# Two of four blocks of x brought in by columns and normalised there by GpSimd, in an attention and MLP block on one core

## The chip, the core and the metric

The kernel runs on one core of a Trainium2 chip. The time is the device time of one execution in microseconds (us). TensorE (PE in the profile, its weight loads PEld) multiplies matrices, VectorE is DVE, ScalarE is ACT, GpSimd is POOL, and SyncE (SP) issues nearly all DMAs. Each engine works through its own instructions in program order and waits on semaphores.

## The reference

x has 2048 rows (tokens) of 448. Cut to what matters:

```python
mod = (silu(c) @ w_mod).reshape(1, 6, 1, 448)          # sa, ca, ga, sb, cb, gb
h = layernorm(x) * (1 + ca) + sa
q, k, v = split_heads(h @ wqkv)                        # 16 heads of 28
p = softmax(q @ k.T * 28 ** -0.5)
x = x + ga * ((p @ v) @ wo)
h = layernorm(x) * (1 + cb) + sb
x = x + gb * (gelu(layernorm(h) @ w1 + b1) @ w2 + b2)  # 448 -> 1792 -> 448
```

Everything is float32. The kernel makes products of nearly that precision out of three faster ones: each operand is split into a rounded part `hi` and a remainder `lo`.

## The kernel before

The work has three stages. The first (to about 163 us) takes x in four blocks of 512 rows. It normalises a block, turns it so that the 448 features lie on partitions, scales and shifts it there by per-partition columns, splits it into hi and lo, and multiplies it with wqkv. The second (163 to 788 us) is attention, in 256 steps; the third is the MLP.

**The turn of a block.** `ln1_stages` (L266) gives eight pieces of work for a block: four take the statistics of 128 rows each on VectorE (`ln_stat`, L208: BN_STATS and BN_AGGR, the last followed by small operations on VectorE and GpSimd), four normalise 128 rows each on ScalarE (L243, L244). Then `h_chunk` (L300) does one of four chunks of 128 features: four TensorE transposes into the PSUM buffer `o` (L287), one ScalarE operation that scales and shifts from there (L308), a ScalarE cast to hi (L292), and a subtraction for lo on GpSimd (L294, L296).

**The tasks of the first stage.** The loop over blocks b runs a list of tasks. A task is eleven matmuls (L407) into one of two `pa` buffers: a group of q or k columns (512 wide), or 128 rows of v (448 wide). ScalarE empties `pa`. After a task's matmuls TensorE runs some products for the softmax's row maxima (L487: 28 rows of q and k, 512 columns), because the attention stage needs each row's maximum before it starts on that row. Each product goes into a PSUM buffer, and VectorE takes its maximum (L492) and so frees it. `mx_ring` hands out these buffers in a fixed cycle of five: ma, ma, m2, m2, m1. A product therefore waits until VectorE is done with the product five places earlier.

**How many products a task gets** is set by `p1_n`. In blocks 1 to 3 a task has five VectorE operations, less those that `emit_mid` (L731) takes. Some of these operations are pairs (`pair_diff`, L496): two products, a Relu on ScalarE (L500) from the first, and one combined VectorE operation (L504, shown as CUSTOM_DVE or ISA) that reads the second. With a pair in the task and `p1_n[1]` true there is one operation more, and the product in the fifth place goes into the buffer `o`. `p1_n[1]` is false where the transposes need `o`. In four tasks of block 1 and one of block 2, `emit_mid` puts four products in the middle of the eleven matmuls. What is not done in the first stage is done in the second, beside the scores.

**Times of the tasks.** I name a task by the microsecond at which its first matmul starts in the trace. Block 1's loop holds eleven tasks, from 55.08 to 97.20. Those with a middle (57.57, 65.30, 73.78, 81.96) have eight products, the others from 61.92 on five or six. The transposes for block 2 stand in the tasks 69.98 to 81.96, those for block 3 in 111.13 to 121.90.

**SP's queue.** SP stores hi and lo of every q and k group to DRAM and copies some rows there (L453, L389), in program order.

## Time and profile before

| | |
|---|---|
| median of three runs | 1090.24 us (1089.82 to 1091.26) |
| the profiled execution, its own time | 1090.18 us |
| its span in the trace | 1088.4 us |
| TensorE busy | 1080.0 us (99%) |
| VectorE, ScalarE, GpSimd busy | 801.5, 696.8, 231.9 us |
| first score matmul of the attention stage | 163.2 us |
| last one starts | 787.9 us |

The profiled execution is 0.06 us below the median. Its span is 1.8 us shorter than its time, for what lies around it. Rows of a timeline give start, length, engine, line, operation, tiles and count; in brackets stands the idle time of the engine before it and what ended it. Rows of windows give, for a stretch A:B, its length and each engine's busy time with its count of instructions. TensorE counts as busy while any of its pipelined matmuls is under way, so a short stall shows less in PE than in the distance between two starts.

### The profile page before, as it was taken

The page shows a single profiled execution, that of the slowest core. Times are in us where ns is not written, and L with a number is a line of the kernel's source. Part 1 is how long each engine was busy: PE and PEld are TensorE (multiplying, and loading weights), DVE is VectorE, ACT ScalarE, POOL GpSimd, SP SyncE. Part 2 cuts the span into 40 slices and gives each one's busy share as a digit, 9 for nine tenths or more (in the row PEclk, how much of TensorE's full clock was granted, in tenths as well). Part 3 has the DMA queues.
Part 4 walks back from the last instruction along what each step waited for, and adds up shares of the span by engine and source line. Part 5 has one row for each costly group of instructions (what it writes and reads, how often), then busy time and mean ns, then how long its engine had stood idle before and what let it go on. Part 6 is the DMA issues. An engine that isn't in the chain of part 4 may idle for free.

```text
span 1088.4 us, 20665 instructions
## 1 busy us (share of the span) xinstructions
PE 1080.0 (99%) x8231; PEld 658.8 (61%) x8231; DVE 801.5 (74%) x1369; ACT 696.8 (64%) x883; POOL 231.9 (21%) x215
## 2 busy tenths in 40 slices
PE   8999999999999999999999999999999999999998
PEld 6766775444444444444444444544388888888887
DVE  6979788999999989988888988584745565464322
ACT  4665658888888888888888888687943321211211
POOL 1543330011011011024231410216114032061000
PEclk9999999999999999999999999999999999999999
DMA  9342272122121202143322423111343311002000
GB/s 312 134 155 76 86 208 88 41 67 58 50 78 59 77 28 58 56 120 87 103 68 77 131 65 96 58 31 59 117 126 96 102 37 41 33 35 73 34 1 34
DMA packets 58870, 88.56 MB, mean 81 GB/s; under 512 B 13807, under 2 KB 25734, under 8 KB 58762
## 3 DMA queue, kind: packets, MB, share of 16 engines
q1 hardware_dynamic: 58290, 86.51, 25.8%
q8 instruction: 64, 1.05, 0.4%
q10 hardware_dynamic: 148, 0.46, 0.1%
q0 software_dynamic: 336, 0.28, 0.1%
q14 instruction: 32, 0.26, 0.1%
HBM read 59.39 MB, written 29.50 MB: 82 GB/s over the span
## 4 chain that ended last, share of the span: by engine, by line
PE 98%; DMA 1%; DVE 1%; ACT 0%; issue 0%; SPq 0%; ACTq 0%
PE s L1393 24%; PE o L1348 24%; PE m L407 17%; PE pa L407 9%; PE m L487 8%; PE s L1485 3%; PE s L1487 3%; PE s L1486 3%; PE s L487 2%; PE t L1487 1%; PE t L1485 1%; PE t L1486 1%; DMA slot_c<-in_w_mod_dram 1%; PE o L287 1%; DVE mxp L492 0%; PE ma L487 0%
## 5 line engine op out<-in xcount | busy, mean ns | idle before, releaser
L492 DVE TENSOR_REDUCE mxp<-m 128x1 f32<-128x512 f32 x553 | 358.1, 686 | 65.0 <-PE m L487 47.7
L1393 PE MATMUL s<-slot_b,slot_a 28*128 28x512 f32 (+1 forms) x3072 | 357.8, 425 | 0.0
L1393 PEld LDWEIGHTS s<-slot_b,slot_a 28*128 28x128 f32 (+1 forms) x3072 | 210.7, 183 | 175.5 <-ACT slot_c L1406 96.4
L487 PE MATMUL m<-kh,qh 28*128 28x512 f32 x606 | 225.8, 469 | 0.8 <-DVE mxp L492 0.3
L1406 ACT ACTIVATE slot_c<-s 128x1024 f32<-128x1024 f32 x170 | 174.8, 1028 | 51.5 <-PE s L1393 50.5
L1348 PE MATMUL o<-slot_c,v 128*32 128x512 f32 x680 | 178.8, 605 | 0.0
L1441 ACT ACTIVATE full<-m,b_col 128x512 f32<-128x512 f32 x56 | 38.6, 690 | 194.2 <-PE m L407 190.0
L698 DVE TENSOR_REDUCE mxp<-s 128x2 f32<-128x1024 f32 x107 | 131.2, 1226 | 5.0 <-PE s L1393 0.3
L1348 PE MATMUL o<-slot_c1h,v 128*32 128x512 f32 x512 | 134.7, 605 | 0.0
L1348 PE MATMUL o<-slot_c0h,v 128*32 128x512 f32 x508 | 133.6, 605 | 0.0
L1406 ACT ACTIVATE slot_c0h<-s 128x1024 f32<-128x1024 f32 x127 | 130.7, 1029 | 0.0
L1406 ACT ACTIVATE slot_c1h<-s 128x1024 f32<-128x1024 f32 x128 | 130.7, 1021 | 0.0
L1406 ACT ACTIVATE slot_d<-s 128x1024 f32<-128x1024 f32 x86 | 88.4, 1028 | 26.1 <-PE s L1393 25.8
L487 PEld LDWEIGHTS m<-kh,qh 28*128 28x128 f32 x606 | 90.4, 182 | 15.4 <-DVE mxp L492 12.7
L1444 DVE CAST hi<-full 128x512 fp32r<-128x512 f32 x42 | 19.2, 458 | 102.0 <-ACT full L1441 101.9
L1068 POOL TENSOR_TENSOR osb<-osb,osb 128x512 f32<-128x512 f32 x16 | 20.6, 1285 | 343.6 <-DMA osb<-drec 282.3
L1348 PE MATMUL o<-slot_d,v 128*32 128x512 f32 x344 | 90.5, 605 | 0.4 <-ACT osb L1312 0.4
L1445 DVE TENSOR_TENSOR lo<-full,hi 128x512 fp32r<-128x512 f32 x56 | 46.2, 825 | 29.7 <-ACT hi L1444 25.7
L407 PE MATMUL m<-y,slot_a 128*128 128x512 f32 x160 | 59.7, 389 | 0.0
L662 DVE CUSTOM_DVE_ANT_0 slot_d0i<-m,slot_d0i 128x512 f32<-128x512 f32 x55 | 38.0, 691 | 16.6 <-PE m L487 14.3
L1348 PEld LDWEIGHTS o<-slot_c,v 128*32 128x32 f32 x680 | 24.5, 108 | 39.7 <-issue 37.8
L492 DVE TENSOR_REDUCE mxp<-ma 128x1 f32<-128x512 f32 x61 | 39.5, 681 | 11.6 <-PE m L487 7.2
(358 smaller groups left out, 1847.1 us busy)
## 6 DMA issues: line engine op xcount, KB each, us to landing
slot_b<-d SPq DMA_DIRECT2D x32, 256.0 KB
slot_a<-d SPq DMA_DIRECT2D x32, 256.0 KB
d<-lo SPq DMA_DIRECT2D x28, 256.0 KB
d<-hi SPq DMA_DIRECT2D x16, 256.0 KB
osb<-drec SPq DMA_DIRECT2D x15, 256.0 KB
out_dram<-xn SPq DMA_DIRECT2D x16, 224.0 KB
raw<-in_B_w_dram SPq DMA_DIRECT2D x14, 224.0 KB
qh<-d SPq DMA_DIRECT2D x12, 256.0 KB
```

Source lines behind the costliest of these rows:

```text
L407: pe.matmul(p, a, b, start=(i == 0), stop=(i == len(terms) - 1))
L487: pe.matmul(m, qh_sb[(g, qt)][js, i * 128 : (i + 1) * 128], k[js, :], start=True, stop=True)
L492: dve.tensor_reduce(out=mxp[(g, qt)][:, i, j, cch : cch + 1], in_=m, op=ALU.max, axis=AX.X)
L698: dve.tensor_reduce(out=mxp[(g, qt)][:, i, j : j + 2, cch], in_=t, op=ALU.max, axis=AX.X)
L1348: pe.matmul(o[32 * j : 32 * j + 32, :], v_sb[kt // 4][:, kt % 4, 4 * g + j, :], p[j // 2][:, j % 2, :], start=(kt == 0), stop=(kt == NKT - 1),
L1393: pe.matmul(s2[:, jj, :], ks[rows_, kp, kc], qs[rows_, qp, :], start=(term == 0), stop=(term == 2))
L1406: act.activation(pt[hf], s2, AF.Exp, scale=SCALE)
L1441: act.activation(gf, p, AF.Gelu_apprx_tanh, bias=b1_col[:, i : i + 1])
L1445: dve.tensor_tensor(out=glo, in0=gf, in1=f(ghi), op=ALU.subtract)
L1485: pe.matmul(pp, ghi[:, ts], w_hi, start=(m == 0), stop=False)
L1486: pe.matmul(pp, ghi[:, ts], w_lo, start=False, stop=False)
L1487: pe.matmul(pp, glo[:, ts], w_hi, start=False, stop=(m == NFT - 1))
```

## The change

Blocks 2 and 3 no longer go through row-wise normalising and transposes. The host hands these rows in a second time, already turned (`x_cols`, feature by feature). The statistics are still taken by rows on VectorE, but two to five tasks earlier in the order. A 128x32 tile of means and reciprocal deviations is turned by one VectorE transpose, sent to DRAM in four small stores, and read back as two tiles in which every partition holds the row of 512 means or deviations. GpSimd then subtracts and multiplies, chunk by chunk (two operations of 128x512 each), in the tasks `APPLY_AT` of the block before. The scaling on ScalarE reads that tile instead of PSUM. As `o` is free of transposes, `p1_n[1]` is true throughout blocks 1 to 3.

```diff
+APPLY_AT = (0, 2, 4, 5)
+    def load_x_cols(b, k):
+        t = xn_t()
+        x_cols[(b, k)] = t
+        if k < 3:
+            sp.dma_start(t, x_t[b - 2, 128 * k : 128 * k + 128, :])
+        else:
+            for h in range(2):
+                sp.dma_start(t[64 * h : 64 * h + 64], x_t[b - 2, 384:D, :])
...
+    def ln1_cols(b):
+        def stat(t):
...
+            ln_stat(mv[0], t, acc[b][:, t, :])
+            if t == 3:
+                st = st32[b % 2]
+                dve.tensor_copy(st[:, 0:4], mv[0][:, :, 0])
+                ve = sbt("ve", [128, 4], bufs=2)
+                dve.tensor_scalar(out=ve, in0=mv[0][:, :, 1], scalar1=EPS, scalar2=None, op0=ALU.add)
+                pool.tensor_tensor(out=st[:, 4:8], in0=ve, in1=neg_half, op=ALU.pow)
+        def rows_out():
+            r = sbt("r32", [128, 32], bufs=2)
+            dve.transpose(r, st32[b % 2])
+            dst = ln_dr[b % 2].rearrange("c (t p) -> (c t) p", p=128)
+            for i in range(4):
+                sp.dma_start(dst[:, 32 * i : 32 * i + 32], r[32 * i : 32 * i + 8, :])
+            for c_ in range(2):
+                sp.dma_start(mr_row(b, c_), ln_dr[b % 2, c_][None].broadcast_to([128, 512]))
+        def apply(k):
+            y = x_cols[(b, k)]
+            pool.tensor_tensor(out=y, in0=y, in1=mr_row(b, 0), op=ALU.subtract)
+            pool.tensor_tensor(out=y, in0=y, in1=mr_row(b, 1), op=ALU.mult)
...
-            p1_n[1] = not (more and (0 <= k < NC)) and not (b == 1 and n < 4)
+            p1_n[1] = bool(b)
...
-                if b and n < 4:
-                    stages[n](xs_next)
+                if b in (1, 2) and n in APPLY_AT:
+                    cols_of[b + 1][1][APPLY_AT.index(n)]()
                 if 0 <= k < NC:
-                    post.append(h_chunk(b + 1, xs_next, k))
-                if later and 7 <= n < 11:
-                    later[n - 7](None)
+                    post.append(h_chunk(b + 1, xs_next, k, x_cols.get((b + 1, k))))
+                n_stat = n - (5, 2, 99)[b]
+                if 0 <= n_stat < 5:
+                    cols_of[b + 2][0][n_stat]()
+                for c_ in {0: range(NC) if n == 10 else (), 1: range(max(0, k - 2), k - 1) if k < NC + 2 else ()}.get(b, ()):
+                    load_x_cols(b + 2, c_)
...
+    x_cols = np.asarray(A_x)[0].reshape(NB, 128, 4, D).transpose(0, 3, 2, 1).reshape(NB, D, 512)[2:]
...
+    nc = bacc.Bacc("TRN2", target_bir_lowering=False, num_devices=1, dynamic_dma_scratch_size=8192)
```

How the order of instructions moves shows at three places. Line numbers of the changed kernel are its own: L492 becomes L549, L504 becomes L561, L487 becomes L544, L407 becomes L464, L210 and L211 become L214 and L215.

The first is VectorE in block 1: all of the task 61.92 and the four middle reductions of the task 65.30. `mxp` holds the maxima; `ma`, `m2`, `m1` and `o` are the PSUM buffers read; the ISA rows are the pair's combined operation. Before:

```order
L492 TENSOR_REDUCE mxp_93_428<-ma_194_842 128x1
L492 TENSOR_REDUCE mxp_93_428<-m2_195_845 128x1
L492 TENSOR_REDUCE mxp_93_428<-m2_196_848 128x1
L504 ISA slot_d0h_15_98,mxp_183_800<-m1_197_851,slot_d0h_15_98 128x512
L504 ISA mxp_183_800 128x1
L492 TENSOR_REDUCE mxp_93_428<-ma_203_873 128x1
L492 TENSOR_REDUCE mxp_93_428<-ma_204_876 128x1
L492 TENSOR_REDUCE mxp_93_428<-m2_205_879 128x1
L492 TENSOR_REDUCE mxp_93_428<-m2_206_882 128x1
```

The same place on VectorE now, in the changed kernel:

```order
L549 TENSOR_REDUCE mxp_97_433<-m2_201_861 128x1
L549 TENSOR_REDUCE mxp_97_433<-m2_202_864 128x1
L549 TENSOR_REDUCE mxp_97_433<-m1_203_867 128x1
L561 ISA slot_d0h_19_102,mxp_190_819<-ma_204_870,slot_d0h_19_102 128x512
L561 ISA mxp_190_819 128x1
L549 TENSOR_REDUCE mxp_97_433<-o_205_873 128x1
L214 BN_STATS st_210_883<-acc3_24_108 128x6
L215 BN_AGGR mv_209_882<-st_210_883 128x2
L549 TENSOR_REDUCE mxp_97_433<-ma_212_898 128x1
L549 TENSOR_REDUCE mxp_97_433<-m2_213_901 128x1
L549 TENSOR_REDUCE mxp_97_433<-m2_214_904 128x1
L549 TENSOR_REDUCE mxp_97_433<-m1_215_907 128x1
```

One reduction (from `o`) and a statistics pair for block 3 now stand ahead of the middle reductions.

The second is TensorE at the end of the task 78.48 and the start of the next, before (`xn` are normalised rows, `pa` the task's result, `ident` the unit matrix):

```order
L487 MATMUL m2_242_1028<-raw_188_814,osb_75_351 128x512
L487 MATMUL m2_243_1031<-raw_188_814,osb_75_351 128x512
L487 MATMUL m1_244_1034<-raw_188_814,osb_75_351 128x512
L487 MATMUL ma_245_1037<-kh0_83_374,qh1_165_717 128x512
L287 MATMUL o_246_1041<-ident_1_77,xn_177_767 128x128
L287 MATMUL o_246_1041<-ident_1_77,xn_191_818 128x128
L287 MATMUL o_246_1041<-ident_1_77,xn_201_858 128x128
L287 MATMUL o_246_1041<-ident_1_77,xn_214_907 128x128
L407 MATMUL pa_248_1050<-slot_e0_34_140,slot_c0_119_523 128x448
```

The same place on TensorE now:

```order
L544 MATMUL ma_256_1068<-raw_91_403,osb_182_783 128x512
L544 MATMUL ma_257_1071<-raw_196_836,osb_79_356 128x512
L544 MATMUL m2_258_1074<-raw_196_836,osb_79_356 128x512
L544 MATMUL m2_259_1077<-kh0_87_379,qh1_173_737 128x512
L544 MATMUL o_260_1080<-raw_91_403,osb_182_783 128x512
L464 MATMUL pa_265_1099<-slot_e0_38_144,slot_c0_125_532 128x448
```

Four transposes are gone, and a product into `o` has come.

The third is VectorE in block 0, the task 33.26 and the first reductions of the task 36.84. Before:

```order
L492 TENSOR_REDUCE mxp_93_428<-m2_112_507 128x1
L492 TENSOR_REDUCE mxp_93_428<-m1_113_510 128x1
L492 TENSOR_REDUCE mxp_93_428<-ma_114_513 128x1
L492 TENSOR_REDUCE mxp_93_428<-ma_115_516 128x1
L446 CAST hi_116_519<-full_117_520 128x512
L492 TENSOR_REDUCE mxp_93_428<-m2_126_556 128x1
```

The same place on VectorE now, from the statistics that stand ahead of it:

```order
L214 BN_STATS st_116_495<-acc2_23_107 128x6
L215 BN_AGGR mv_115_494<-st_116_495 128x2
L503 CAST hi_112_488<-full_113_489 128x512
L549 TENSOR_REDUCE mxp_97_433<-m2_118_516 128x1
L549 TENSOR_REDUCE mxp_97_433<-m1_119_519 128x1
L549 TENSOR_REDUCE mxp_97_433<-ma_120_522 128x1
L549 TENSOR_REDUCE mxp_97_433<-ma_121_525 128x1
L214 BN_STATS st_131_543<-acc2_23_107 128x6
L215 BN_AGGR mv_115_494<-st_131_543 128x2
L503 CAST hi_122_528<-full_123_529 128x512
L549 TENSOR_REDUCE mxp_97_433<-m2_133_568 128x1
```

Block 2's first two statistics pairs have moved here; before, they stood behind the tasks 36.84 and later.

## The prediction

> **What bounds the kernel now.** The page first: the span, who is busy, and the chain of waits that ended last.

> ```profile
> span 1088.4 us, 20665 instructions
> PE 1080.0 (99%) x8231; PEld 658.8 (61%) x8231; DVE 801.5 (74%) x1369; ACT 696.8 (64%) x883; POOL 231.9 (21%) x215
> PE 98%; DMA 1%; DVE 1%; ACT 0%; issue 0%; SPq 0%; ACTq 0%
> ```

> TensorE carries the chain almost throughout, so a TensorE instruction that goes should shorten the kernel. But the page is an average, and a pipelined engine can look busy while it waits. So I read the windows next, cut at the starts of the tasks of the first stage; the columns are length, then busy time (and count) of PE, PEld, DVE, ACT and POOL.

> ```profile
> 61.92:65.30 3.38, 3.38 (x17) 2.28 (x16) 2.01 (x6) 2.35 (x6) 1.02 (x1) 1.00 0.59 213
> 65.30:69.98 4.68, 4.68 (x20) 2.65 (x19) 4.68 (x9) 2.72 (x6) 1.57 (x2) 1.00 0.44 163
> 61.92:69.98 8.06, 8.06 (x36) 4.92 (x35) 6.69 (x14) 5.07 (x11) 2.58 (x2) 1.00 0.50 184
> 69.98:78.48 8.50, 8.44 (x44) 5.71 (x43) 7.09 (x15) 5.93 (x12) 4.11 (x5) 1.00 0.46 170
> 78.48:86.91 8.43, 8.10 (x45) 5.71 (x44) 6.85 (x15) 4.91 (x9) 2.57 (x2) 1.00 0.21 32
> 86.91:90.00 3.09, 3.09 (x20) 2.29 (x18) 2.34 (x7) 1.53 (x3) 1.15 (x1) 1.00 0.21 26
> 90.00:100.94 10.94, 10.94 (x53) 7.38 (x51) 10.87 (x23) 4.76 (x9) 2.71 (x3) 1.00 0.26 90
> 104.37:107.76 3.39, 3.39 (x19) 2.28 (x18) 2.51 (x7) 3.21 (x8) 1.53 (x2) 1.00 0.41 156
> 111.13:121.90 10.77, 10.77 (x62) 8.01 (x60) 7.91 (x17) 8.55 (x17) 6.42 (x8) 1.00 0.46 168
> 121.90:130.30 8.40, 8.23 (x43) 5.50 (x41) 7.42 (x15) 5.20 (x11) 2.57 (x2) 1.00 0.01 3
> 728.53:742.39 13.86, 13.86 (x105) 8.88 (x101) 8.89 (x20) 8.09 (x10) 4.60 (x4) 1.00 0.01 2
> 742.39:746.76 4.37, 4.37 (x32) 2.67 (x32) 0.79 (x4) 2.48 (x3) 3.40 (x3) 1.00 0.03 6
> ```

> In block 1 a plain task (61.92) leaves VectorE free for over a third of its 3.38 us, while a task with products in its middle (65.30) has VectorE busy for all of its 4.68. The timeline of these two shows who ends what.

> ```profile
> 61.92 1.20 PE L407 MATMUL pa<-slot_c,slot_a 128*128 128x512 f32 x4
> ...
> 64.64 0.50 PE L487 MATMUL ma<-raw,qh 28*128 28x512 f32 x1
> ...
> 65.21 0.69 DVE L492 TENSOR_REDUCE mxp<-ma 128x1 f32<-128x512 f32 x1 [1.37 <-PE m L487]
> ...
> 67.02 0.68 DVE L504 CUSTOM_DVE_ANT_0 slot_d0h<-m,slot_d0h 128x512 f32<-128x512 f32 x1
> ...
> 67.62 1.28 DVE L492 TENSOR_REDUCE mxp<-ma 128x1 f32<-128x512 f32 x2
> ...
> 68.82 1.28 DVE L492 TENSOR_REDUCE mxp<-m 128x1 f32<-128x512 f32 x2
> ...
> 69.56 0.50 PE L487 MATMUL m<-kh,qh 28*128 28x512 f32 x1
> 69.98 1.21 PE L407 MATMUL pa<-slot_c,slot_a 128*128 128x512 f32 x4
> ```

> VectorE starts 3.29 after the plain task does (65.21 - 61.92), takes one product each 0.60 (four by 67.62), then the middle's. The last product of the task with a middle goes into the buffer of the middle's third product, counted five back in the cycle. That one's reduction starts at 68.82 and ends 0.68 later; the product follows at 69.56, the next task 0.42 after it. So two tasks take 3.29 + 4 x 0.60 + (2 x 0.60 + 0.68) + 0.48 = 8.05; the window says 8.06. **In block 1 VectorE's in-order work sets the pace, not TensorE's.** The chain puts that stretch down to TensorE all the same.

> **The change part by part.** The sum is made against the profiled execution, 1090.18 us, which is 0.06 below the median of the runs.

> First, VectorE in block 1. In each plain task `p1_n[1]` adds a reduction, in each task with a middle a product at the end, which now needs the buffer of the middle's fourth product. That is 2 x 0.60 per two tasks. The first task with a middle (57.57) begins with VectorE idle and pays one step, +0.6. The statistics, too, come earlier; their price is the start of BN_STATS to that of the next reduction:

> ```profile
> 45.86 0.62 DVE L210 BATCH_NORM_STATS2 st<-acc 128x6 f32<-128x448 f32 x1
> ...
> 46.61 1.25 DVE L492 TENSOR_REDUCE mxp<-ma 128x1 f32<-128x512 f32 x2
> ```

> 0.75 each. Those in the tasks 61.92 and 69.98 stand ahead of the middle's reductions and cost it in full; those behind the tasks with a middle fall where VectorE waits for the next products. So the pair of tasks from 61.92 takes 8.05 + 1.20 + 0.75 = 10.0, **+1.9** on 8.06. The pair from 69.98 has the same list, 10.0, against 8.50: **+1.5**. It loses transposes on the way; their price:

> ```profile
> 77.66 0.50 PE L487 MATMUL ma<-kh,qh 28*128 28x512 f32 x1
> ...
> 78.09 0.66 PE L287 MATMUL o<-ident,xn 128*128 128x128 f32 x4
> ...
> 78.51 1.06 PE L407 MATMUL pa<-slot_e,slot_c 128*128 128x448 f32 x4
> ```

> 0.42 for four, on the path behind a middle, beside VectorE's work elsewhere. The pair from 78.48 has no statistics now but the 128x32 transpose (0.2, as other small operations), and as v tasks are 0.3 shorter it comes to 3.0 + 3.0 + 0.2 + 1.8 + 0.68 + 0.48 = 9.2, **+0.7** on 8.43. The three tasks from 90.00 lose their statistics and should take 3.39 each, as 104.37 does with the same six products: 10.2, **-0.8** on 10.94. Block 1 in sum: 0.6 + 1.9 + 1.5 + 0.7 - 0.8 = **+3.9**. Bounds: +2.4 if the two statistics found a gap after all, +4.6 if the last three tasks gained nothing.

> Second, block 0. There VectorE is just ahead of TensorE's need, and two statistics pairs move in front of these reductions (the tasks 33.26 and 36.84):

> ```profile
> 37.34 1.27 DVE L492 TENSOR_REDUCE mxp<-m 128x1 f32<-128x512 f32 x2
> ...
> 38.54 1.27 DVE L492 TENSOR_REDUCE mxp<-ma 128x1 f32<-128x512 f32 x2
> ...
> 39.28 0.50 PE L487 MATMUL m<-kh,qh 28*128 28x512 f32 x3
> ```

> With one pair ahead, the third reduction (38.54) starts at 39.29 and ends at 39.97. The fourth product of 36.84 reuses that buffer and is due at 39.3: a stall of 0.7. The second pair adds a few tenths in the two tasks after. I take **+1.1**, between 0 (the lag is absorbed) and 1.5 (two pairs in full).

> Third, block 2. Its transposes stand in plain tasks, where TensorE does set the pace. The three tasks 111.13 to 121.90 become one like 104.37 and two like 86.91: 3.39 + 2 x 3.09 = 9.6 against 10.77, **-1.2**, though each does one product more. The stretch from 121.90 gains nothing: its second task has a middle, the reductions before it stay four, and 8.4 is the sum of the first part again (3.0 + 2.4 + 4 steps). ScalarE: a second Relu per task,

> ```profile
> 65.18 0.60 ACT L500 ACTIVATE slot_d0h<-ma 128x512 f32<-128x512 f32 x1 [1.03 <-PE m L487]
> ```

> gives 8.55 + 3 x 0.60 = 10.35 in 9.6, so it ends up to 0.8 late; I take **+0.3**, between 0 and 0.8. The 16 normalising operations that ScalarE loses lie mostly ahead of this and are worth nothing by themselves: ScalarE is busy 5.93 of 8.50 us at most in block 1.

> Fourth, attention. The ten products done earlier end the row maxima sooner, in the steps with a projection: three steps with products take 13.86, one without takes 4.37, so 13.86 - 3 x 4.37 = **-0.75** (0 to -1.2, with one more step beside them).

> Fifth, what is hidden. GpSimd gets 16 operations; a two-input operation of 128x512 there costs

> ```profile
> L1068 POOL TENSOR_TENSOR osb<-osb,osb 128x512 f32<-128x512 f32 x16 | 20.6, 1285 | 343.6 <-DMA osb<-drec 282.3
> ```

> 1.285 each, 20.6 in all, 2.6 per chunk. GpSimd is busy 2.57 to 4.11 of each 8.4 us in block 1, and a chunk is applied two to four tasks ahead of its use: zero. SP issues 22 more DMAs; behind the loads that wait for the rows are only stores that are read tens of us later: zero. The smaller descriptor scratch meets three GpSimd DMAs that follow one on another: zero.

> Sum: 3.9 + 1.1 - 1.2 + 0.3 - 0.75 = **+3.35**, so 1090.18 + 3.35 = **1093.5 us**.

> **The rivals.** *A, TensorE's saving comes through.* If VectorE caught up everywhere, eight groups of four transposes (0.42) and 0.75 in attention would go: 1090.18 - 3.4 - 0.75 = 1086.0. For it speaks the chain (PE 98%), and that six products cost TensorE no more than five (104.37: 3.39, 61.92: 3.38); against it the DVE column at 65.30. Chance 0.13.

> *B, they cancel.* The statistics find gaps (block 0 +0, block 1 +2.4): 3.35 - 1.1 - 1.5 = +0.75, 1090.9. Chance 0.15.

> *C, GpSimd's queue stalls on the rows.* The first chunk's subtraction is queued ahead of the clearing of `mxp` (61.44), for which VectorE's pair operations wait.

> ```profile
> 58.11 1.29 POOL L450 TENSOR_TENSOR lo<-full,kh 128x512 fp32r<-128x512 f32 x1
> ...
> 61.44 0.15 POOL L484 MEMSET mxp<- 128x64 f32 x1
> ```

> ```profile
> osb<-drec POOLq DMA_DIRECT2D x1, 256.0 KB, 6.3
> den<-osb POOLq DMA_DIRECT2D x1, 8.0 KB, 3.7
> ```

> It decides whether the rows have landed by 59.4, when GpSimd is free. The statistics are turned at about 51 (four reductions from 46.61, some 1.6 late); stores and loads at 3.7 and 6.3, with 1.2 of issue, land at about 62. At 6.3 for both it would be 65, the clearing 2.6 + 1.3 later, at 69, and VectorE would lose about 4: 1097.5. [...] Chance 0.08.

> *D, GpSimd and VectorE hold each other up.*

> ```profile
> 29.28 0.42 DVE L446 CAST raw<-full 128x512 fp32r<-128x512 f32 x1
> ...
> 29.37 1.47 POOL L450 TENSOR_TENSOR lo<-full,osb 128x512 fp32r<-128x512 f32 x1
> ```

> Beside a VectorE cast a subtraction took 1.47, not 1.29. If each of the 16 cost VectorE as much, 16 x 0.18 = 2.9 would come on top: 1096.4. [...] Chance 0.05.

> That the change does not do what it says is no rival: the order shows the 32 transposes gone.

> **How the numbers follow.** The forecast has 0.59; its own range, from its terms' bounds, is 1090.5 to 1096. About 0.2% (2.2 us, so 1088.1 and 1092.4) is what can be told from no change. Faster: A, 0.13. Same: B and the low end of the forecast, 0.15 + 0.10 = 0.25. Slower: 0.49 + C + D = 0.62. The range 1088.5 to 1097.0 leaves out A and most of C, 0.2 together.

> **What would show it.** Right: between the starts of the tasks that were 57.57 and 90.00 the changed profile takes some 4.7 us more, tasks with a middle last about 6 us with VectorE busy throughout, the three tasks of block 2 last 9.6, and the maxima end at the step before the projections. Wrong: tasks with a middle under 5 us with VectorE idle in them (A or B), a VectorE wait on GpSimd's clearing near 64 (C), or reductions longer than 0.7 beside GpSimd's work (D).

## The result and the profile after

| | before | changed |
|---|---|---|
| median of six runs each | 1090.0 us (1089.8 to 1091.26) | 1098.3 us (1096.37 to 1100.07) |
| ratio, with its 95% interval | | 1.0074 (1.0061 to 1.0087) |
| the profiled execution, its own time | 1090.18 us | 1100.07 us |
| its span | 1088.4 us | 1098.3 us |
| first score matmul of attention | 163.2 us | 170.9 us |

Slower, as forecast, but by 8.3 us and not by 3.35: 1098.3 lies above the range, which ended at 1097.0. The profiled execution is the slowest of its six. The six differ in the mean clock that TensorE was granted:

| run, us | 1096.37 | 1097.13 | 1097.68 | 1098.91 | 1099.15 | 1100.07 |
|---|---|---|---|---|---|---|
| mean clock | 0.999 | 0.998 | 0.998 | 0.996 | 0.996 | 0.994 |

In the fourteen profiles of this document a mean of 0.998 or less goes with at least one stretch of half clock in the middle of the kernel (a drop, from here on), and 0.999 or 1.000 with none. By that reading five of these six executions have a drop. Of the 68 executions of the kernel before that were run beside the experiments none has: all have 0.999 or 1.000.

The page of the changed kernel gives a row for the clock, in tenths by 40 slices, and the chain of waits:

```profile
PE 1088.0 (99%) x8199; PEld 660.5 (60%) x8199; DVE 800.7 (73%) x1373; ACT 692.1 (63%) x871; POOL 251.8 (23%) x231
PEclk9998999999999999999999999999999999999999
PE 95%; DVE 3%; issue 0%; DMA 0%; ACT 0%; ACTq 0%; DVEq 0%
```

The chain now has 3% of VectorE where it had 1%. TensorE has 32 matmuls less and is busy 8 us longer, and the fourth slice of the clock shows an 8, in a row that was all nines before. The windows, cut at the same tasks as the prediction's (58.99 is the old 57.57, 63.94 the old 61.92, then the pairs of 69.98 and 78.48, the tasks 86.91 and 90.00, the three of block 2 from 111.13, the stretch from 121.90, the task 130.30; behind the busy times stand the granted clock, the DMA share and GB/s):

```profile
58.99:63.94 4.95, 4.84 (x22) 2.73 (x20) 2.96 (x5) 2.14 (x4) 4.87 (x5) 1.00 0.87 322
63.94:73.92 9.98, 8.99 (x38) 5.23 (x37) 8.57 (x18) 4.15 (x8) 5.92 (x6) 1.00 0.51 185
73.92:84.19 10.27, 9.87 (x38) 5.70 (x37) 9.59 (x21) 5.16 (x9) 8.73 (x9) 0.92 0.32 116
84.19:94.92 10.73, 10.42 (x38) 6.87 (x37) 8.12 (x20) 3.49 (x7) 4.00 (x4) 0.76 0.00 0
94.92:98.01 3.09, 3.09 (x19) 2.31 (x17) 2.60 (x7) 1.34 (x3) 1.29 (x1) 1.00 0.49 125
98.01:108.35 10.34, 10.34 (x53) 7.33 (x52) 9.32 (x19) 4.48 (x9) 3.10 (x3) 1.00 0.47 135
118.52:128.07 9.55, 9.55 (x53) 6.85 (x52) 7.52 (x19) 8.23 (x16) 7.94 (x10) 1.00 0.58 217
128.07:136.52 8.45, 8.17 (x40) 5.17 (x38) 7.83 (x17) 7.07 (x13) 5.68 (x5) 1.00 0.03 9
136.52:141.47 4.95, 4.95 (x18) 3.41 (x17) 1.39 (x6) 0.13 (x1) 0.00 (x0) 0.66 0.00 0
```

Lengths at full clock come out as forecast: 4.95, 9.98 (10.0), 9.55 (9.6), 8.45 (8.4). Those with a clock under 1.00 do not: 10.27 where 10.0 was forecast, 10.73 where 9.2 was, and the task 136.52, in which VectorE is busy for 1.39 us and ScalarE and GpSimd hardly at all, takes 4.95 instead of 3.38. The same trace cut where the clock changes, and into stretches of the length of the shorter drop ahead of that:

```profile
72.22:75.63 3.41, 3.11 (x10) 1.97 (x11) 3.41 (x7) 1.67 (x3) 1.64 (x2) 1.00 0.26 98
75.63:79.04 3.41, 3.41 (x19) 1.93 (x17) 2.77 (x8) 1.87 (x4) 2.52 (x4) 1.00 0.29 101
79.04:82.46 3.42, 3.02 (x11) 1.77 (x10) 3.39 (x9) 1.89 (x5) 2.92 (x3) 1.00 0.40 153
82.46:89.28 6.82, 6.82 (x20) 4.53 (x19) 4.39 (x12) 1.41 (x3) 4.35 (x4) 0.50 0.03 10
89.29:92.70 3.41, 3.30 (x19) 2.08 (x14) 3.24 (x8) 2.35 (x4) 0.81 (x1) 1.00 0.00 0
133.66:137.07 3.41, 3.13 (x11) 1.55 (x10) 3.41 (x6) 1.79 (x4) 1.27 (x1) 1.00 0.00 0
137.07:140.48 3.41, 3.41 (x9) 2.63 (x8) 0.78 (x4) 0.00 (x0) 0.00 (x0) 0.50 0.00 0
```

Half clock for 6.82 and 3.41 us, and ahead of each a stretch of 3.41 in which TensorE ran only 11 matmuls (19 in a full one) while VectorE was busy for nearly all of it. Not every such stretch brings a drop: the one from 72.22 has 10, and the clock stays. What decides it can't be read from these rows. The two drops start 54.61 us apart, 16 times 3.413. The profile of the last experiment has three: 6.83 us at 0.50 from 83.29, and, as the clocks of its windows give it, two that start 13.7 and 61.5 us later, 4 and 18 times 3.413 (13.65 and 61.44) within the rounding of those clocks. So in these two profiles the drops start on a step of about 3.41 us. Counted from the start of the execution, it lies at another place in each: 82.46 is 24 such steps and 0.54 us, 83.29 is 24 steps and 1.37 us.

The timeline of TensorE there shows a stall on VectorE and, from 82.88, the same kind of product taking 0.79 instead of 0.49. Two rows of waits, for the task 77.30 to 84.19 (total, times, longest), show what its weight loads waited for, VectorE's reductions:

```profile
80.99 0.49 PE L544 MATMUL m<-raw,qh 28*128 28x512 f32 x1
81.68 1.25 PE L544 MATMUL ma<-raw,osb 28*128 28x512 f32 x2 [0.20 <-DVE mxp L549]
82.88 0.79 PE L544 MATMUL m<-raw,osb 28*128 28x512 f32 x1
83.47 0.79 PE L544 MATMUL m<-kh,qh 28*128 28x512 f32 x1
```

```profile
PEld m L544 <- DVE mxp L549: 1.1, 3, 0.4
PEld ma L544 <- DVE mxp L549: 0.9, 2, 0.5
```

Attention, from the start of its first step to that of its last, takes 625.7 instead of 624.0. The three steps with a projection gained what was forecast, 13.05 against 13.86:

```profile
738.81:751.86 13.05, 13.05 (x94) 8.02 (x94) 1.94 (x6) 8.16 (x10) 4.55 (x4) 1.00 0.01 2
```

But the step where the list of products now ends takes 3.82, with 2.2 in its neighbours. Its last product waits for VectorE (TensorE's rows, then VectorE's):

```profile
733.88 0.40 PE L544 MATMUL s<-kh,qh 28*128 28x512 f32 x1
735.06 0.49 PE L544 MATMUL s<-kh,qh 28*128 28x512 f32 x1 [0.78 <-DVE mxp L549]
```

```profile
734.32 0.69 DVE L549 TENSOR_REDUCE mxp<-s 128x1 f32<-128x512 f32 x1
```

Where no pair of products is left for one reduction, two single ones go into the halves of one buffer `s`, and the second is held until the first is reduced.

Where the 9.9 us between the two spans are: 0.2 ahead of the first task, 1.2 in block 0, 6.0 in block 1, 0.35 in block 2 (-1.2 and +1.57), -0.1 in block 3, 1.7 in attention, 0.5 behind it. The 0.2 need not belong to the change: in the fourteen profiles the first task starts between 23.35 and 24.82.

### The profile page after: what moved, and what is told of

Its sections match the earlier page's. It is cut to its first block, busy times and chain, and to the rows that moved or that the text cites. A ratio compares the mean times of both kernels' runs of the same rounds, so it can differ in the third digit from the quotient of the medians.

```text
span 1098.3 us, 20640 instructions
## 1 busy us (share of the span) xinstructions
PE 1088.0 (99%) x8199; PEld 660.5 (60%) x8199; DVE 800.7 (73%) x1373; ACT 692.1 (63%) x871; POOL 251.8 (23%) x231
## 4 chain that ended last, share of the span: by engine, by line
PE 95%; DVE 3%; issue 0%; DMA 0%; ACT 0%; ACTq 0%; DVEq 0%
PE s L1453 23%; PE o L1408 23%; PE m L464 16%; PE pa L464 8%; PE m L544 7%; PE s L1545 3%; PE s L1547 3%; PE s L1546 3%; DVE mxp L549 2%; PE s L544 2%; PE t L1547 1%; PE t L1545 1%; PE t L1546 1%; PE ma L544 1%; PE pa L385 0%
## 5 line engine op out<-in xcount | busy, mean ns | idle before, releaser
L549 DVE TENSOR_REDUCE mxp<-m 128x1 f32<-128x512 f32 x546 | 353.2, 686 | 65.6 <-PE m L544 42.3
L544 PE MATMUL m<-kh,qh 28*128 28x512 f32 x594 | 220.8, 471 | 0.7 <-ACT full L840 0.3
L757 DVE TENSOR_REDUCE mxp<-s 128x2 f32<-128x1024 f32 x105 | 128.7, 1226 | 4.6 <-PE s L544 0.3
L544 PEld LDWEIGHTS m<-kh,qh 28*128 28x128 f32 x594 | 88.2, 182 | 17.0 <-DVE mxp L549 14.6
L464 PE MATMUL m<-y,slot_a 128*128 128x512 f32 x160 | 59.7, 389 | 0.0
L544 PE MATMUL s<-kh,qh 28*128 28x512 f32 x212 | 47.7, 439 | 0.8 <-DVE mxp L549 0.8
## 6 DMA issues: line engine op xcount, KB each, us to landing
slot_b<-d SPq DMA_DIRECT2D x32, 256.0 KB
slot_a<-d SPq DMA_DIRECT2D x32, 256.0 KB
d<-lo SPq DMA_DIRECT2D x28, 256.0 KB
d<-hi SPq DMA_DIRECT2D x16, 256.0 KB
osb<-drec SPq DMA_DIRECT2D x15, 256.0 KB
qh<-d SPq DMA_DIRECT2D x12, 256.0 KB
```

Source lines behind the costliest of these rows:

```text
L464: pe.matmul(p, a, b, start=(i == 0), stop=(i == len(terms) - 1))
L544: pe.matmul(m, qh_sb[(g, qt)][js, i * 128 : (i + 1) * 128], k[js, :], start=True, stop=True)
L549: dve.tensor_reduce(out=mxp[(g, qt)][:, i, j, cch : cch + 1], in_=m, op=ALU.max, axis=AX.X)
L757: dve.tensor_reduce(out=mxp[(g, qt)][:, i, j : j + 2, cch], in_=t, op=ALU.max, axis=AX.X)
```

## The experiments

Two theories at the start. V: VectorE's in-order work sets the pace of block 1, as forecast, and on top of that the stalls it causes make TensorE's clock drop. Against it G (GpSimd's new work, through its queue or by holding VectorE up; the port named for it in the expectations is a guess, which no view shows) and K (the drops are chance or belong to the layout). Intervals are 95%, and each ratio is to the kernel before, which was run beside it, at 1089.6 to 1090.4. The edits are cut to what matters and the comments in them are mine; `n` counts the tasks of a block's loop from 0.

**Five operations in block 1.**

```diff
-            p1_n[1] = bool(b)
+            p1_n[1] = b > 1
```

> The changed kernel with one line back: no sixth product in block 1 (its tasks take five operations as before), block 2 keeps six. Theory V (VectorE's in-order work sets the pace of block 1; the clock drops of TensorE follow from its stalls there): block 1 loses one step of 0.60 in the first task with a middle and two in each of the three pairs behind it, 4.2 us, and with the shorter stalls the clock drop near 82 us (about 3 us in the profiled execution) mostly goes; the ten late products of attention end as before, another 0.7. At full clock 1095.4 - 4.2 - 0.7 = 1090.5, with a drop left in block 2 up to 1092: 1090 to 1092.5. Rival G (GpSimd's new work or its port costs the time): stays at 1096 to 1099. Rival K (the clock drops are chance, unrelated to the stalls): clock between 0.994 and 0.999 as in the changed kernel.

1091.27 us, ratio 1.0011 (1.0003 to 1.002). Clock 1.000. The three pairs of block 1:

```profile
61.87:70.65 8.78, 8.66 (x37) 5.10 (x36) 7.47 (x16) 4.05 (x8) 6.49 (x7) 1.00 0.57 205
70.65:79.44 8.79, 8.48 (x36) 5.23 (x35) 8.10 (x18) 4.70 (x10) 7.29 (x8) 1.00 0.38 139
79.44:87.83 8.39, 7.61 (x36) 4.95 (x35) 8.03 (x20) 4.60 (x9) 5.45 (x5) 1.00 0.03 8
```

9.98 - 2 x 0.60 = 8.78: two steps of VectorE, to the hundredth, in the first two pairs. The third lost 0.59 of 1.2 (8.98 at full clock, 8.39 here): in it TensorE waited 0.69 for a Relu on ScalarE. All of GpSimd's work is still there, so G falls for the most part. None of the eleven executions has a drop. One line gives back 7 of the 8.3 us.

**Block 3's statistics late.**

```diff
-                n_stat = n - (5, 2, 99)[b]
+                n_stat = n - (5, 7, 99)[b]        # rows out with the fourth, applied from n = 3
```

> The changed kernel with block 3's statistics back at the end of block 1 (n = 7 to 10, the rows sent out with the last), applied in block 2 from n = 3. Theory V: the pairs from the tasks with the old starts 61.92 and 69.98 lose 0.75 each, the next 0.2, the last three tasks of block 1 take 0.6 back: 1.1 less, and fewer clock drops; median 1095.5 to 1097.3. Rival S (statistics find gaps): no change, 1098.3 within 0.7. Rival G: no change either.

1098.2 us, ratio 1.008 (1.0067 to 1.0093): no gain, which the theory had not expected. The parts:

```profile
63.68:72.95 9.27, 8.49 (x38) 5.02 (x38) 7.90 (x16) 3.47 (x7) 5.93 (x6) 1.00 0.54 194
106.66:111.41 4.75, 4.53 (x19) 2.73 (x18) 3.56 (x12) 3.21 (x7) 2.29 (x2) 1.00 0.32 111
```

The pair did lose 0.71, so the price of a statistics pair ahead of the middle holds. But the task 106.66 takes 4.75 instead of 3.38: the transpose of the rows stood right behind the statistics, and VectorE waited 1.1 us in it for GpSimd's small operation. And the clock dropped once all the same. A wait that this edit added took back most of the gain.

**Products issued twice.**

```diff
-        pe.matmul(m, ...)
+        for _ in range(1 + hot[0]):      # hot: tasks with a middle, all products but the last
+            pe.matmul(m, ...)
```

> The changed kernel with work added: in the five tasks with a middle every product but the last is issued twice into the same buffer, so TensorE is busy where it waited. Theory V with the clock following TensorE's activity: no drop of the granted clock (0.999 or 1.000 in every run), VectorE's pace unchanged, so faster by adding work: 1095.5 within 1, and runs that agree within 1.5 us. Rival K (the drops are chance or follow from something else): clock 0.994 to 0.999 as in the changed kernel, 1098 to 1100. Rival T (TensorE is the bound there): about 37 more products at 0.215 us, up to 8 us more, 1106.

1095.97 us (1095.73 to 1096.34), ratio 1.0058 (1.0045 to 1.0071): 2.3 us faster than the changed kernel by adding work. No drop in the profile; the last two pairs and the task behind block 2's middle:

```profile
73.15:83.12 9.97, 9.97 (x46) 6.16 (x45) 9.30 (x20) 5.15 (x10) 8.40 (x9) 1.00 0.32 119
83.12:92.10 8.98, 8.98 (x46) 6.00 (x45) 8.81 (x22) 3.90 (x8) 4.31 (x4) 1.00 0.01 1
133.70:137.07 3.37, 3.37 (x19) 2.29 (x18) 1.41 (x6) 0.45 (x2) 0.00 (x0) 1.00 0.00 0
```

VectorE's pace is what it was, and the lengths are those of full clock: 9.97, 8.98, 3.37 against 10.27, 10.73, 4.95. So the drops cost 0.30 + 1.75 + 1.58 = 3.6 in the profiled execution of the changed kernel. All five executions here have a mean clock of 0.999 or 1.000.

**Without GpSimd's 16 operations.**

```diff
-            pool.tensor_tensor(out=y, in0=y, in1=mr_row(b, 0), op=ALU.subtract)
-            pool.tensor_tensor(out=y, in0=y, in1=mr_row(b, 1), op=ALU.mult)
```

> The changed kernel without GpSimd's 16 operations: x goes into the products without mean and deviation taken off in blocks 2 and 3 (that part of the computation is left out); all else stays. Theory V: GpSimd's work is hidden, 1098.3 within 0.8, the tasks with a middle as long as before. Rival G (GpSimd holds VectorE up by its port or its queue): 2.9 to 4 less, 1094 to 1095.5.

1096.68 us (1095.07 to 1100.89), ratio 1.007 (1.0057 to 1.0083). The median is between the two expectations and settles nothing, since here too the clock dropped, twice in the profile. Executions of equal mean clock (0.998) are closer than G allows: 1096.64 and 1096.73 here, 1097.13 and 1097.68 in the changed kernel. The undisturbed pair settles it:

```profile
63.21:73.19 9.98, 8.51 (x38) 5.07 (x37) 8.57 (x18) 4.14 (x8) 2.56 (x2) 1.00 0.50 183
```

9.98 with GpSimd's 5.92 us of work, 9.98 with 2.56. The first task with a middle is 4.95 in both, the three tasks of block 2 are 9.57 here and 9.55 there. G is out for the places at which the changed kernel has this work.

**Before with the smaller descriptor scratch.**

```diff
-    nc = bacc.Bacc("TRN2", target_bir_lowering=False, num_devices=1)
+    nc = bacc.Bacc("TRN2", target_bir_lowering=False, num_devices=1, dynamic_dma_scratch_size=8192)
```

> The kernel before with nothing changed but the smaller descriptor scratch of GpSimd's DMAs (8192). In the changed kernel and in its variants the attention stage and what follows took 926.9 to 927.6 us against 925.2, some 1.0 of it in small steps spread over the first half of attention. Theory R (the scratch does it, since GpSimd issues DMAs there): 1.0 to 1.9 more, 1091. Theory L (the list of the maxima that are left for attention does it): no change, 1089.8 within 0.4.

1089.93 us, ratio 1.0002 (0.9994 to 1.0011). No cost.

**The old rule, so attention's old list.**

```diff
-            p1_n[1] = bool(b)
+            p1_n[1] = not (more and (0 <= k < NC)) and not (b == 1 and n < 4)
```

> The changed kernel with the old rule for p1_n[1]: no product is added anywhere, so attention has the list of before. Left are the column layout, GpSimd's work and the earlier statistics. Theory V: stage 1 as in the run with five operations in block 1, no drop of the clock. Theory L: attention and the rest back to 925.2, the median 1.0 to 1.9 under that run: 1089.3 to 1090.3. Theory R, or a cost of the layout itself: 1091.3 as in that run, the rest at 927.

1090.97 us (1089.94 to 1093.04), ratio 1.0011 (1.0003 to 1.002), between the two expected; the clock dropped once in the profiled execution (3.4 us of half clock behind the last middle of block 1, whose next task took 4.47 instead of 3.09). The median does not separate the theories; the steps do. Attention's steps 16 to 127 take 278.8 in before, 278.8 with the small scratch, 278.6 here, but 280.0 in the changed kernel and 279.8 with five operations in block 1. So the list of the maxima left for attention costs the 1.0 to 1.2 in these steps, not the scratch nor the layout. But attention and what follows did not come back to 925.2, as theory L had it: they take 926.3. The steps 128 to 229 take 241.2 instead of 240.4, nearly all of it in the steps 188 to 192, and 0.5 is added behind attention. Neither can come from the list, which is the old one here. The layout isn't ruled out for them, and their cause stays open.

**Five operations, all statistics at the old places.**

```diff
-                n_stat = n - (5, 2, 99)[b]
+                n_stat = n - (7, 7, 99)[b]        # rows out with the fourth, applied from n = 3
```

> Five operations in block 1, and both blocks' statistics at the old places (n = 7 to 10 of the block two ahead), the rows sent out with the last of them, applied from n = 3. Theory V: against the run with five operations alone block 0 loses 1.2 (no statistics ahead of its reductions), the pairs from the old starts 61.92 and 69.98 0.7 each, the three last tasks of block 1 take 0.8 back: about 1.9 less, 1089.4, just under the kernel before. Rival C (the rows come too late, GpSimd waits for them and holds up the clearing of the maxima): a task of block 1 with TensorE waiting on GpSimd, 1091 or more.

1090.09 us, ratio 1.0003 (0.9995 to 1.0012); 0.7 over the forecast. Block 0 lost its 1.2 (12.67, as before), the pairs are at 8.07 and 8.10. But the task 99.16 takes 4.20 instead of 3.4, as VectorE waits for GpSimd in front of the transpose here as well, and the stretch of block 2 that ends with the middle takes 8.93 where the run with five operations alone has 7.85: GpSimd's operations come so late there that ScalarE waits 2.2 us for them. GpSimd's work is not hidden wherever it is put.

```profile
99.00 0.16 DVE L319 TENSOR_SCALAR ve<-mv 128x4 f32<-128x4 f32 x1
100.28 0.21 DVE L324 STREAM_TRANSPOSE r<-st 128x32 f32<-128x32 f32 x1 [1.13 <-POOL st L320]
```

**Twice, with a new end of the list.**

```diff
-            emit_single(half, lambda: t[:, jj])
+            emit_single(half, (lambda: t[:, 0], ps_mx)[jj])
```

> The changed kernel with the products of its tasks with a middle issued twice (no clock drop), and one line more: where no pair of products is left at the end of the list, the second single product takes a PSUM buffer of its own instead of the other half of the first one's. If the 3.82 us of attention step 230 (2.2 in its neighbours) is that wait, the step falls to 2.2 to 2.5 and the median from 1095.97 to 1094.5 within 0.3; if not, nothing changes.

1096.25 us (1094.47 to 1097.33), ratio 1.0055 (1.0041 to 1.0068). The step falls from 3.82 to 2.97, half of the way. The median, over the expected 1094.5, shows nothing, as three of the five executions have a mean clock of 0.998, the profiled one with a drop; the one with 1.000 took 1094.47. Issuing twice makes drops rarer (3 of the 10 executions of these two runs have 0.998, 5 of 6 of the changed kernel 0.998 or less) and does not exclude them.

**Statistics only where VectorE waits.**

```diff
-                n_stat = n - (5, 2, 99)[b]
-                if 0 <= n_stat < 5:
-                    cols_of[b + 2][0][n_stat]()
+                stat_at = ((7, 8, 9, 10, 11), (3, 5, 7, 8, 9), ())[b]
+                if n in stat_at:
+                    cols_of[b + 2][0][stat_at.index(n)]()
```

with the old rule for `p1_n[1]`, and GpSimd's operations at n = 2 to 5.

> The changed kernel with the old rule for p1_n[1] (attention's list as before) and the statistics put only where VectorE waits anyway: block 2's at the old place (n = 7 to 10 of block 0, the rows sent out a task later), block 3's behind the tasks with a middle (n = 3, 5, 7) and at n = 8, rows out at n = 9; GpSimd applies in the tasks n = 2 to 5. Theory V: block 0 as before, no stall from statistics in block 1, so the transposes' saving comes through: the pairs 8.06 to 8.1 (0.4 less from 69.98, 0.35 less from 78.48), the last three tasks of block 1 0.7 less, block 2 1.2 less, no clock drop; 0.5 more behind the last matmul as in all variants: 1089.55 - 2.65 + 0.5 = 1087.4, 1086.8 to 1088.2. Rival (rows too late, or statistics cost 0.75 wherever they stand): 1089 or more.

1088.08 us (1087.33 to 1088.61), ratio 0.9982 (0.9973 to 0.9991): faster than the changed kernel and by 0.18% faster than before. The pairs of block 1 and the three tasks of block 2:

```profile
62.10:70.17 8.07, 8.07 (x37) 4.93 (x36) 6.70 (x14) 3.34 (x7) 6.39 (x6) 1.00 0.72 268
70.17:78.26 8.09, 7.94 (x36) 4.95 (x35) 7.40 (x16) 4.66 (x9) 7.69 (x8) 1.00 0.55 202
78.26:86.30 8.04, 7.60 (x36) 4.96 (x36) 7.59 (x17) 5.00 (x10) 5.19 (x5) 1.00 0.43 138
110.42:119.98 9.56, 9.56 (x50) 6.84 (x48) 7.53 (x17) 7.35 (x14) 9.40 (x11) 1.00 0.53 195
```

8.06, 8.50, 8.43 and 10.77 before. Statistics behind a middle cost nothing (with none in them, in the run with all statistics at the old places, the pairs took 8.07, 8.10 and 8.04), and what the transposes cost comes through: 0.4 in each of two pairs, 1.2 in block 2. The last three tasks of block 1 did not give their 0.7: they take 10.89 against 10.94, as the last statistics stand ahead of the reductions of the task 92.90, which takes 4.02. The 0.5 behind attention, which I had put in, is not there in this run nor in the next; it stays unexplained.

**Statistics behind all four middles.** As above with `(1, 3, 5, 7, 8)` for block 1, and the applies of block 2 as in the change.

> As the run before it, but block 3's statistics behind all four tasks with a middle (n = 1, 3, 5, 7), rows out at n = 8, applied in block 2 at n = 0, 2, 4, 5 as in the changed kernel. Theory V: 1087.4 too, with the task 100.94 (old start) not lengthened by rows that come late; 1086.8 to 1088.2. Rival as in the run before: 1089 or more.

1095.63 us, ratio 1.0054 (1.0041 to 1.0067), far over the forecast. The pairs are 8.07, 8.07 and 8.03, and then one task of block 2 takes 8.85 instead of 3.4, with a clock drop behind it. SP's queue, then GpSimd's:

```profile
91.98 1.30 SPq L327 DMA_DIRECT2D ln_dr<-r  x4
95.57 0.82 SPq L329 DMA_DIRECT2D slot_v<-ln_dr  x2
97.68 3.11 SPq L458 DMA_DIRECT2D ones_d<-slot_d  x1
100.83 4.29 SPq L510 DMA_DIRECT2D d<-qh  x1
105.17 3.36 SPq L510 DMA_DIRECT2D d<-lo  x1
```

```profile
111.65 1.28 POOL L507 TENSOR_TENSOR lo<-full,hi 128x512 fp32r<-128x512 f32 x1 [8.71 <-DMA d<-lo]
```

The rows' loads stand in SP's queue ahead of a store of constants (L458) and the stores of hi and lo. Those came so late that GpSimd had to wait for its buffer `lo`; behind it in its queue stood the clearing of `mxp`, for which VectorE waited 6.1 and TensorE 5. The changed kernel issues the same stores from 103.01 and 105.29, and there GpSimd doesn't wait. This chain is read from the trace. No run moved the store of constants alone.

**Products issued three times.** As the run with two, `1 + 2 * hot[0]`.

> The changed kernel, in its five tasks with a middle every product but the last issued three times into the same buffer (the run with two had no clock drop in its profile and agreed within 0.6 us; the run with two and the new end of the list spread over 2.9 us and had a drop in its profile, so two may only make drops rarer). A third issue fills VectorE's 0.60 us per product almost wholly: three at 0.215. Clock by TensorE's activity: no drop, runs within 1.0 us of each other, 1096.0 to 1097.0 (0.3 to 0.6 more in the first such task, where VectorE has no backlog). Rival K (the drops are chance): spread of 2 us or more, clock of the profile under 0.999, 1097 to 1100.

1097.2 us (1096.57 to 1098.45), ratio 1.0065 (1.0051 to 1.0079). Clock 1.000 in the profile, all pairs at full-clock length, the last 9.42 with the extra work. The spread of 1.9 is over the 1.0 expected because of one execution, 1098.45, whose mean clock is 0.997: by the reading above it has a drop, so three issues do not exclude drops either. The other four lie within 0.75. Products issued twice or three times come to 4 executions of 15 with 0.998 or less, the changed kernel to 5 of 6.

**Before, the middle's reductions done twice.**

```diff
-        dve.tensor_reduce(out=..., in_=m, op=ALU.max, axis=AX.X)
+        for _ in range(1 + slow[0]):      # slow: in emit_mid
+            dve.tensor_reduce(out=..., in_=m, op=ALU.max, axis=AX.X)
```

> The kernel before, with every reduction of the products in the middle of a task done twice (20 reductions more, nothing else). Theory V: the product that closes such a task waits for three more steps of 0.60, and the next plain task takes up to one step more: 1.8 to 2.4 for each of the five, 9 to 12 in all, 1098.8 to 1101.8 at full clock; TensorE then stands still long enough for the clock to drop as in the changed kernel, 1.5 to 4 more, with half clock in the profile right behind such a task. Rival T (TensorE sets the pace, VectorE has time): 1090 to 1091. Rival K (the drops come from the column layout): full clock throughout, 1.000.

1106.65 us (1104.07 to 1108.57), ratio 1.0149 (1.0131 to 1.0166), clock 0.991. Where the clock is whole, the pace is as forecast: the first task with a middle is 2.2 longer, the pair behind it 2.2 (10.22 against 8.06). Then it drops, three times 6.8 us, in a kernel without any of the change:

```profile
64.03:74.25 10.22, 8.63 (x37) 5.12 (x36) 9.46 (x18) 5.09 (x11) 2.58 (x2) 1.00 0.33 121
74.25:85.51 11.26, 9.61 (x43) 6.37 (x43) 10.41 (x20) 3.88 (x8) 4.12 (x5) 0.90 0.31 111
98.80:104.14 5.34, 5.34 (x19) 4.02 (x19) 2.47 (x7) 1.53 (x3) 1.27 (x1) 0.53 0.00 0
146.27:152.05 5.78, 5.78 (x20) 3.89 (x18) 2.42 (x7) 0.13 (x1) 0.00 (x0) 0.54 0.00 0
```

The drops cost more than the 4 I allowed. All four executions have a mean clock of 0.991 to 0.995. With this K is out: slow VectorE work alone makes the clock drop (all four here, none of the 68 of the kernel before), and more TensorE work makes drops rarer (4 of 15 against 5 of 6).

## Why the prediction was right in its direction and wrong in its size

| term | forecast | measured |
|---|---|---|
| block 0 | +1.1 | +1.2 (12.67 to 13.87 in the four tasks concerned) |
| block 1, at full clock | +3.9 | +3.9 |
| block 2, plain tasks | -1.2 | -1.2 |
| ScalarE in block 2 | +0.3 | none in the three tasks (9.55); 0.05 in the stretch behind them (8.45 against 8.40) |
| attention | -0.75 | +1.7 |
| clock drops | none | +3.6 in the profiled execution |
| ahead of the first task, behind attention | none | +0.2, +0.5 |

Block 1 at full clock is put together from two profiles: 4.95 and 9.98 of the changed kernel, 9.97 and 8.98 of the run with products issued twice, then 3.09 and 10.34, in sum 47.31 against 43.37 before. So VectorE's pace, its 0.60 a step and 0.75 for statistics, and the place of the statistics were right, each also by a run that changed it. Of the signs that were named, the three tasks of block 2 last 9.55, the maxima end ahead of the projections, and the first undisturbed task with a middle behind a plain one lasts 5.65 with VectorE busy for 5.62. But between the starts of 57.57 and 90.00 the profile has 39.02 against 32.43, 6.6 more and not 4.7; 4.5 of that is what these rows make at full clock, the rest is drops.

Two small things in the working were wrong without harm. The lower bounds of the terms give 1090.2, not 1090.5. And ScalarE was to have 10.35 us of work in 9.6; it has 8.23, since two Relus were added in this stretch and not three, and one normalisation of 1.2 us, which fell away, had stood in it (at 112.44).

**The steps that failed** are two: a term for the clock, which wasn't there, and the term for attention, which had the wrong sign (-0.75, measured +1.7). The sum was made "against the profiled execution", whose clock is 1.00 in every quoted row, and none of the rivals asked what the stalls of 0.60 per product, which it put into block 1, do to the clock. That cost the 3.6 us of drops in the profile. These last 6.82 and 3.41 us at a clock of 0.50, each behind a stretch of 3.41 us in which TensorE ran 11 matmuls. Why the clock falls there, and why the six executions differ in it, isn't shown. Of the 8.3 us between the medians some 2 to 2.5 are drops: 2.5 by the run with products issued twice (1095.97, of which 0.2 is its own extra work), 1.9 by the one execution of the changed kernel with a mean clock of 0.999 (1096.37). Either failed term alone is enough to leave the range: without the drops the median would be near 1096, with attention as forecast near 1095.9.

**Attention** was forecast as the end of the list alone. That part came (13.86 to 13.05). Two costs of the same move were left out: the list now ends with an odd remainder that waits on itself (step 3.82 against 2.2, shown in the trace and half mended by one line), and it is another list all the way, 1.0 to 1.2 in the steps 16 to 127, which the run with the old list doesn't have. Why another list costs that much in these steps isn't known. Had I counted what the planner makes of a shorter list, the sign of this term would have been open.

**The rivals.** A did not happen in the changed kernel, since VectorE didn't catch up; in part it did where the statistics were moved behind the middles, with 2.0 of the 3.4 us that A gave the transposes. C named a time close to the measured one by luck: the first subtraction started at 60.79 without a wait, as the rows, loaded on SP's queue from 53.52, had landed by then. Its mechanism is real all the same: it came with block 3's rows in the run with statistics behind all four middles, through SP's queue, which the prediction had dismissed as "only stores that are read tens of us later". They were read late, but their buffers were wanted back early. D is refuted by the pair of 9.98 with and without GpSimd's work. The chances of C and D, 0.08 and 0.05, were my estimates, and no row of the prediction makes them that low. But "zero" for GpSimd holds only for where the change puts its work, as the run with all statistics at the old places shows.

## What to carry to other kernels

Work taken from an engine that the chain of waits names is worth nothing where another engine's in-order queue sets the pace: look at a stretch of a few us, add up that queue's steps, and put new work only behind the point where it waits. Before a change that makes TensorE stand more often, count its matmuls in stretches as long as the shorter drop (3.41 us here) as well: a row of stalls of a few tenths came with 10.2 us of half clock in the profiled execution, which cost 3.6, and with a mean clock of 0.994 to 0.999 in the six, though no limit on the count came out of these runs. And a list that a planner works off is a part of the change: look at how it ends.
